# Five shared PSUM banks and joint score visits in a fused attention and expert kernel

## The chip, the cores and the metric

One core of one Trainium2 chip. The metric is the device time in microseconds (us) of a run, lower is better; beside it stands one profiled execution with a trace of every instruction.

## The reference

Attention with a memory term, then a gated expert layer on its rows, all in float32:

```
a     = softmax(q k^T / 8, causal) v              # B=4, H=8, S=576, D=64
mem   = phi(q) M_prev / (phi(q) z_prev + 1e-6)    # phi(x) = x+1 if x>0 else exp(x)
x     = sigmoid(beta) mem + (1 - sigmoid(beta)) a # -> 2304 rows x 512
out   = (sigmoid(x w_gate) * (x w_val)) w_out     # d_ff = 1536
```

## The kernel before

**Units.** The rows of x are handled in six groups of 384. Groups 1 to 4 are the first 384 rows of one batch each; groups 0 and 5 (called tail) hold the last 192 rows of two batches. A group has four pairs of heads, so there are 24 `pairs`, 0 to 23. A full pair has two items: scores of 128 queries against 256 keys, and of 384 and 128 keys together. A tail pair has three: two of 512 keys and a "mixed chunk" of 576 keys, which is done in two parts, of 320 and 256.

**Attention of a pair.** `scores` multiplies q and k on TensorE (PE) in small tiles (64x64 or 64x128 of the array, several side by side; line L523), and in the first part's banks also the memory terms phi(q) M (`terms`, L480). Such a row of small-tile matmuls among the big products is called a visit below. DVE masks the scores and takes their maximum (L587, an operation followed by a short read of its accumulator), ACT takes the exponential (L599). `turn` brings the result into key-major order: for the first eight pairs by transposes on PE (L285) and copies on ACT (L291), for the rest by a DMA transpose of two 16-bit planes, which DVE makes and joins (`planes`, L612). Of a tail pair's 512 or 576 keys a DMA transpose takes four blocks of 128; the fifth, of the mixed chunk, goes by PE transposes and an ACT copy. `values` (L282) multiplies by v for a couple of pairs, `recall` and `scaled` divide, DVE adds the memory term (`xs<-xs,xm`, L301), and `across` makes the transposed `xh` and `xl`: float32 numbers are split in two halves of PE's faster fp32r format, and each product is three matmuls.

**Experts.** `moe` runs eight stages; each step of a stage takes 128 of the 1536 columns f: 12 products of 384 columns for the gate, 12 for the value (`bank<-xh,wg`, `bank<-xh,sv`), then ACT's tanh (L920), DVE's product of gate and value (L922), the split (`gh`, `gl`), and nine products of 512 columns into three accumulators (`down`). Weights are prepared once by `convert` (ACT L810, DVE L812, L814, L817) and stored.

**Banks.** PSUM has eight banks. 0 to 2 hold the accumulators. After the first stage attention takes turns on 5, 6 and 7, and gate and value on 3 and 4.

**What sets the order.** Nothing is issued directly: the program is recorded as operations with a cost each (`pg.add`), and `issue()` schedules them in a list by these costs, by their dependencies, and by an order number, to which the table `MOVED` adds an offset for chosen operations. `block()` keeps PE operations together. The costs and the table belong to the kernel's text, and so decide the order on every engine, and which bank an operation gets is decided when it is recorded.

Of the kernel before, what the change touches and what calls it, by code (L numbers as in the profile page):

```python
# [27 lines left out]


# [174 lines left out]
def tile_attention_memory_moe(  # L204
# [60 lines left out]
    turns = {"att": 0, "gv": 0, "second": 0}  # L265
# [21 lines left out]
    def act(n, emit, r, w):  # L287
        pg.add("act", 0.09 + n / 1200.0, emit, r, w)
# [4 lines left out]
    def dve(n, emit, r, w, fast=False):  # L293
        pg.add("dve", 0.065 + n / (1920.0 if fast else 960.0), emit, r, w)
# [200 lines left out]
    def split(n):  # L495
# [10 lines left out]
        for e, (kp, kk) in enumerate(u.kp):  # L506
            for j in range(2):
# [3 lines left out]
                copy(kq[h, used], kp[h, used], used.stop, [kk], [kh])  # L511
                copy(kq[l, qs], kp[h, qs], nq, [kk], [kd])
                sub(nc.vector, kq[l, ks], kp[h, ks], kq[h, ks].bitcast(F32), nk, [kk, kh], [kl])
                q = ql[j][0][:, e * nq:(e + 1) * nq]
                sub(nc.vector, q[h], kp[h, qs], kq[h, qs].bitcast(F32), nq, [kk, kh], [kx])
# [11 lines left out]
    def scores(n, x):  # L527

        u = pairs[n]
        pair = u.tail and x == 2  # L530
        js = [slice(64 * j, 64 * j + 64) for j in range(2)]
        a = [a_r.take() for _ in js]
        if pair:
            _, q0, W = u.items[x][0]
            parts = [[(0, 0, 320)], [(0, 320, W)]]
        else:
            parts = [[(i, 0, W) for i, (_, _, W) in enumerate(u.items[x])]]
        st = [[st_r.take() for _ in js] for _ in u.items[x]]

        def part(i, cells):  # L540
            sp = [bank("att") for _ in js]
            more = pair and i == 1 or not u.tail and x == 0
            work, at = [], 0
            for y, k0, k1 in cells:
                c, q0, W = u.items[x][y]
                if pair:
                    es = [(0, 128, 0, 64), (1, 128, 64, 128)]
                    mk, mk_k = (mask2[:, :k1 - k0], "mask2") if i else (mask[:, :k1 - k0], "mask")
                else:
                    es = [(c if u.tail else 0, q0, 0, 128)]  # L550
                    if more:
                        es = [(0, q0, 0, 64), (0, q0 + 64, 64, 128)]
                    mk, mk_k = mask[:, 512 - W:], "mask"
                work.append((y, es, k0, k1, at, mk, mk_k))
                at += k1 - k0
            if more:
                u.told = [(sp[j][0][:, at:at + 3 * MC].rearrange("p (c j x) -> p c j x", c=3, j=1),
                           sp[j][1], j, j + 1) for j in range(2)]

            def together():  # L560
# [5 lines left out]
            with pg.block():  # L566
                if not divided(u) or pair:
                    e_ = {e for _, es, *_ in work for e, *_ in es}
                    pe(4 * at / 2385.0 + (0.36 if more else 0.32), together,
# [23 lines left out]
        for i, cells in enumerate(parts):  # L593
            part(i, cells)
# [283 lines left out]
    def moe(n):  # L878
# [20 lines left out]
        for at, f in enumerate(fs):  # L899
# [29 lines left out]
            if prev:  # L929
                yield from down(*prev)  # L930
# [134 lines left out]
```

## Time and profile before

| | |
|---|---|
| median of 3 runs | 610.99 us (610.62 to 611.63) |
| the profiled execution's own time | 611.24 us |
| its span | 609.5 us |
| PE busy | 598.1 us, 98% |
| DVE busy | 459.0 us, 75% |
| ACT busy | 309.9 us, 51% |
| first product of the expert layers (L278) starts | 48.25 us |
| the last one starts | 604.55 us |

Sums are made against the profiled execution; 1.7 us of its time lie outside the span. "Busy" counts the time in which an engine works on something; matmuls overlap in the pipeline, so the pace of a stretch is read from the starts of its rows, not from their lengths.

### The profile page before, as it was taken

To read this page: it belongs to the slowest core of one execution; us is meant where nothing else is said; L and a number is where in the kernel's file an instruction comes from. 1 tells how busy PE (TensorE), PEld (TensorE's weight loads), DVE (VectorE), ACT (ScalarE), POOL (GpSimd) and SP (SyncE) were. 2 spreads that over 40 slices of the span, in tenths; PEclk is the share of its full clock that TensorE was granted. 3 is DMA by queue.
4 is the path that set the end of the run, shared out by engine and by line. 5 is a ranking of instruction groups with operands and counts; after the bars stand their busy time and mean duration, and the time that the engine had idled before them with its cause. 6 is when DMAs were issued, how large, how long until landed. Compare 5 with 4: busy or idle time off the path is not lost.

```text
span 609.5 us, 13288 instructions
## 1 busy us (share of the span) xinstructions
PE 598.1 (98%) x5184; PEld 528.4 (87%) x5184; DVE 459.0 (75%) x1181; ACT 309.9 (51%) x620; POOL 8.4 (1%) x51
## 2 busy tenths in 40 slices
PE   7899999999999999999999999999999999999997
PEld 3589888888999988989888989889889888999996
DVE  4899999999998566667686867787989999333432
ACT  6987978455665232342452553463746554223332
POOL 2000000000000000000000000000000000000000
PEclk9999999999999999999999999999999999999999
DMA  8777676999594454764684653776778666222231
GB/s 319 238 230 248 188 220 215 218 242 298 150 293 157 125 136 106 154 123 108 163 168 110 131 130 95 173 185 140 154 152 202 162 123 152 48 66 90 71 103 53
DMA packets 111535, 98.17 MB, mean 161 GB/s; under 512 B 79984, under 2 KB 82032, under 8 KB 111472
## 3 DMA queue, kind: packets, MB, share of 16 engines
q1 hardware_dynamic: 111328, 97.05, 61.3%
q8 instruction: 41, 0.67, 0.5%
q10 hardware_dynamic: 144, 0.26, 0.1%
q14 instruction: 22, 0.18, 0.1%
HBM read 65.84 MB, written 12.58 MB: 129 GB/s over the span
## 4 chain that ended last, share of the span: by engine, by line
PE 94%; ACT 2%; DVE 1%; DMA 1%; SPq 1%; issue 0%; POOL 0%
PE bank L278 77%; PE bank L282 8%; PE bank L523 6%; PE bank L285 3%; PE bank L480 1%; DMA vt<-in_vp_dram 1%; ACT a L599 1%; SPq L309 1%; ACT at L291 1%; DVE a L587 0%; DVE wt L814 0%; DVE wt L817 0%; DVE xs L301 0%; DVE wt L812 0%; DVE sv L301 0%
## 5 line engine op out<-in xcount | busy, mean ns | idle before, releaser
L278 PE MATMUL bank<-xh,wg 128*128 128x384 f32 x576 | 165.2, 341 | 0.0
L278 PE MATMUL bank<-xh,sv 128*128 128x384 f32 x576 | 163.1, 338 | 0.0
L278 PE MATMUL bank<-sv,gh 128*128 128x512 f32 x432 | 139.5, 398 | 0.0
L278 PEld LDWEIGHTS bank<-xh,wg 128*128 128x128 f32 x576 | 105.5, 188 | 4.7
L278 PEld LDWEIGHTS bank<-xh,sv 128*128 128x128 f32 x576 | 105.4, 188 | 2.2 <-issue 1.0
L278 PE MATMUL bank<-xl,wg 128*128 128x384 f32 x288 | 97.4, 338 | 0.0
L278 PE MATMUL bank<-xl,sv 128*128 128x384 f32 x288 | 97.2, 338 | 0.0
L922 DVE SCALAR_TENSOR_TENSOR th<-th,bank 128x384 f32<-128x384 f32 x72 | 39.6, 550 | 76.4 <-PE bank L278 71.6
L612 DVE COPY at<-a 128x1024 uint16<-128x1024 uint16 (+1 forms) x144 | 87.0, 623 | 6.8 <-ACT a L599 3.1
L599 ACT ACTIVATE a<-a,st 128x512 f32<-128x512 f32 (+3 forms) x144 | 77.8, 582 | 26.5 <-DVE st L587 26.1
L278 PEld LDWEIGHTS bank<-sv,gh 128*128 128x128 f32 x432 | 79.2, 188 | 12.3
L920 ACT ACTIVATE th<-bank 128x384 f32<-128x384 f32 x72 | 35.3, 491 | 105.3 <-PE bank L278 102.4
L278 PE MATMUL bank<-sv,gl 128*128 128x512 f32 x216 | 84.7, 395 | 0.0
L291 ACT CAST gh<-th 128x384 fp32r<-128x384 f32 x72 | 36.9, 513 | 89.2 <-DVE th L922 88.8
L587 DVE CUSTOM_DVE_ANT_0 a<-bank,mask 128x512 f32<-128x512 f32 (+3 forms) x144 | 64.6, 483 | 20.4 <-PE bank L523 12.8
L278 PEld LDWEIGHTS bank<-xl,wg 128*128 128x128 f32 x288 | 54.1, 188 | 3.8 <-issue 1.0
L523 PE MATMUL bank<-kp 64*64 64x256 f32 (+4 forms) x416 | 51.5, 442 | 5.0 <-DMA kp<-in_qk_dram 4.1
L278 PEld LDWEIGHTS bank<-xl,sv 128*128 128x128 f32 x288 | 54.1, 188 | 1.0
L301 DVE TENSOR_TENSOR sv<-sv 128x512 fp32r<-128x512 f32 x84 | 54.3, 686 | 0.0
L301 DVE TENSOR_TENSOR gl<-th,gh 128x384 fp32r<-128x384 f32 x72 | 39.9, 554 | 16.9 <-ACT gh L291 16.8
L291 ACT CAST sv<-sv 128x512 fp32r<-128x512 f32 x84 | 47.7, 616 | 5.2 <-DMA sv<-w 5.2
L278 PEld LDWEIGHTS bank<-sv,gl 128*128 128x128 f32 x216 | 40.5, 188 | 8.8
(67 smaller groups left out, 598.2 us busy)
## 6 DMA issues: line engine op xcount, KB each, us to landing
sv<-w SPq DMA_DIRECT2D x42, 512.0 KB, 4.0
wr<-in_w_dram SPq DMA_DIRECT2D x36, 512.0 KB, 4.6
kp<-in_qk_dram SPq DMA_DIRECT2D x32, 384.0 KB, 3.7
w<-wt SPq DMA_DIRECT2D x24, 256.0 KB, 4.5
out_dram<-ob SPq DMA_DIRECT2D x14, 256.0 KB, 2.0
vt<-in_vp_dram SPq DMA_DIRECT2D x8, 330.0 KB, 4.4
vr<-in_vp_dram SPq DMA_DIRECT2D x8, 330.0 KB, 4.9
mb<-in_mz_dram SPq DMA_DIRECT2D x8, 260.0 KB, 4.7
```

Source lines behind the costliest of these rows:

```text
L278: lambda: nc.tensor.matmul(out=out, lhsT=lhsT, rhs=rhs, start=start, stop=stop), r, w)
L282: lambda: nc.tensor.matmul(out=out, lhsT=lhsT, rhs=rhs, start=start, stop=stop), r, w)
L285: pe(0.110, lambda: nc.tensor.transpose(out=out, in_=in_, identity=identity), r, w)
L291: act(n, lambda: nc.scalar.copy(out=out, in_=in_), r, w)
L301: dve(n, lambda: nc.vector.tensor_tensor(out=out, in0=in0, in1=in1, op=op), r, w)
L309: pg.add("sp", 0.5, lambda: nc.sync.dma_start(out=out, in_=in_), r, w, kb)
L523: nc.tensor.matmul(out=sp[j][0][m0:m1, at:at + k1 - k0], lhsT=kp[r, u.qa + q:u.qa + q + m1 - m0], rhs=kp[r, u.ka + k0:u.ka + k1], start=Tr ...
L587: dve(m + 10, lambda aj=aj, sj=sj, pj=pj, o=o, m=m, mk=mk, b=b0 + k0: nc.vector.tensor_tensor_reduce(out=aj[:, b:b + m], in0=pj[:, o:o + m ...
L599: act(W + 120, lambda aj=aj, sj=sj, b=b0, W=W: nc.scalar.activation(out=aj[:, b:b + W], in_=aj[:, b:b + W], func=AF.Exp, scale=-1.0, bias= ...
L612: dve(2 * W, lambda: nc.vector.tensor_copy(out=o, in_=i), r, w, fast=True)
L920: act(GT, lambda: nc.scalar.activation(out=th, in_=pg_[:, :GT], func=AF.Tanh, scale=0.5), [pg_k], [th_k])
L922: dve(GT, lambda: nc.vector.scalar_tensor_tensor(out=th, in0=th, scalar=1.0, in1=pv[:, :GT], op0=ALU.add, op1=ALU.mult,), [th_k, pv_k], [t ...
```

## The change

- `bank()` draws from one stock. From the second stage on attention, gate and value share banks 3 to 7; a list `taken` marks the two that gate and value hold until the gate's operations are recorded.
- `joint(n)` writes both items' scores and the memory terms of a full pair in one visit of 64x64 tiles, over four banks. `attn` calls it where the stock has five banks, and waits for `taken` to be empty. In the built program these are pairs 10 to 19; pairs 4 to 9 keep their two visits.
- The last four mixed chunks (pairs 20 to 23) have both parts and the terms in one visit.
- The values of a couple are one unit of the planner.
- The fifth key block of the last four pairs goes by the DMA transpose (`crossed`): eight transposes of 10x128 instead of 8x128, 16 DVE copies of 1280 instead of 1024 elements, eight pads on POOL more; eight PE transposes and four ACT copies less.
- The last 128 rows of the last step: their products are done in two halves of 256 columns in banks of their own, ACT copies the accumulator ahead, and DVE adds each half, which goes out by a DMA of its own.
- The planner's costs and the whole table `MOVED` are new, so the order is planned anew from the start.

```diff
-        ids = {"att": att_banks, "gv": [3, 4], "second": [0, 1]}[kind]
-        turns[kind] += 1
-        t, k = banks[ids[(turns[kind] - 1) % len(ids)]]
+        if kind == "second" or kind == "gv" and len(att_banks) == 3:
+            i = {"second": 0, "gv": 3}[kind] + turns[kind] % 2
+            turns[kind] += 1
+        else:
+            i = next(i for i in att_banks if i not in taken)
+            att_banks.remove(i)
+            att_banks.append(i)
+            if kind == "gv":
+                taken.append(i)
+        t, k = banks[i]
...
-        pe(0.004 + max(n, 128) / 2250.0,
+        pe(0.0055 + max(n, 128) / 2250.0,
-        pg.add("act", 0.09 + n / 1200.0, emit, r, w)
+        pg.add("act", 0.102 + n / 1200.0, emit, r, w)
-        pg.add("dve", 0.065 + n / (1920.0 if fast else 960.0), emit, r, w)
+        pg.add("dve", 0.083 + n / (1920.0 if fast else 960.0), emit, r, w)
...
+    def joint(n):
+
+        u = pairs[n]
+        js = [slice(64 * j, 64 * j + 64) for j in range(2)]
+        sp = [[bank("att") for _ in js] for _ in u.items]
...
+        for x, cells in enumerate(u.items):
+            at = 0
+            for y, (_, q, W) in enumerate(cells):
+                work.append((x, y, [(0, q, 0, 64), (0, q + 64, 64, 128)], W, at))
+                at += W
+        end = sum(W for _, _, W in u.items[0])
+
+        def together():
+            for x, _, es, W, at in work:
+                heads(u, es, sp[x], js, 0, W, at)
+            terms(u, sp[0], js, end)
...
+        plain = [job for job in jobs if not divided(u) or job[0] == 2]
+        with pg.block():
+            for some in [plain] * (n >= HP and plain != []) or [[job] for job in plain]:
...
-        n = min(nb, 4)
-        W = 128 * n
+        W = 128 * nb
...
-                scores(n, x)
+                if x == 0:
+                    pairs[n].whole = not pairs[n].tail and len(att_banks) == 5
...
+                elif not pairs[n].whole:
+                    while (taken or len(att_banks) == 3) and pairs[n].tail and x == 2:
+                        yield "wait"
+                    scores(n, (x,))
+                elif x == 0:
+                    yield from turned(1)
+                    while taken:
+                        yield "wait"
+                    joint(n)
...
+                last = g == NG - 1 and t == order[2]
+                terms = (gh, (wh, wh_k)), (gh, (wl, wl_k)), (gl, (wh, wh_k))
+                if last and f == fs[-1]:
+                    for h in (0, DM // 2):
+                        b, bk = bank("att")
+                        for i, ((l, l_k), (r, r_k)) in enumerate(terms):
+                            matmul(b[:, :DM // 2], l[:, ts], r[:, h:h + DM // 2], DM // 2, [l_k, r_k], [bk], i == 0, i == 2)
...
+                    dve(DM // 2, lambda o=o, b=b: nc.vector.scalar_tensor_tensor(
+                        out=o, in0=b[:, :DM // 2], scalar=0.5, in1=o, op0=ALU.mult, op1=ALU.add), [bk, ok], [ok])
+                    engine, queue = (("sp", nc.sync), ("act", nc.scalar))[h]
...
+        if n == 1:
+            att_banks[:] = range(3, 8)
```

PE, pair 11 (buffer `kp_106`), before: the 256-column item with its terms, and some 200 rows later the 384/128 item. Banks 63 to 65 are the accumulators, 66 and 67 gate and value, 68 to 70 attention's; each score row stands here once for its kind.

```order
L278 MATMUL bank_64<-sv_149,gl_153 128x512
L278 MATMUL bank_66<-xh_134,wg_95 128x384
L523 MATMUL bank_69<-kp_106 64x256
L523 MATMUL bank_70<-kp_106 64x256
L480 MATMUL bank_69<-mb_108,ph_128 64x65
...
L278 MATMUL bank_63<-sv_139,gh_152 128x512
L523 MATMUL bank_68<-kp_106 128x384
L523 MATMUL bank_69<-kp_106 128x384
L523 MATMUL bank_68<-kp_106 128x128
L523 MATMUL bank_69<-kp_106 128x128
L278 MATMUL bank_63<-sv_139,gh_152 128x512
```

PE, the same pair after the change. Banks 67 and 68 are those that the products of value and gate have just filled; the last gate product is the first row.

```order
L289 MATMUL bank_68<-xh_157,wg_99 128x384
L289 MATMUL bank_63<-sv_139,gh_155 128x512 x2
L289 MATMUL bank_63<-sv_139,gl_156 128x512
L289 MATMUL bank_64<-sv_139,gh_155 128x512
L534 MATMUL bank_70<-kp_106 64x256
L534 MATMUL bank_66<-kp_106 64x256
...
L534 MATMUL bank_67<-kp_106 64x384
L534 MATMUL bank_68<-kp_106 64x384
...
L534 MATMUL bank_67<-kp_106 64x128
L534 MATMUL bank_68<-kp_106 64x128
...
L491 MATMUL bank_70<-mb_108,ph_128 64x65
...
L289 MATMUL bank_64<-sv_139,gh_155 128x512
```

Both items are one piece, on banks 70 and 66 first and then on 67 and 68, three rows of products (four instructions) behind the last gate product.

DVE in the opening, before: conversions of the first weights (`wt`, lines L812, L814, L817) around the addition for pair 0 (`xs_132`). Line numbers after the change are L876, L878 and L881.

```order
L812 TENSOR_SCALAR wt_141<-wt_141 128x512
L814 SCALAR_TENSOR_TENSOR wt_141<-wr_140,wt_141 128x512
L462 SCALAR_TENSOR_TENSOR rs_133<-bank_66,ga 128x6
L817 SCALAR_TENSOR_TENSOR wt_141<-wr_140,wt_141 128x512
L466 RECIPROCAL rs_133<-rs_133 128x6
L812 TENSOR_SCALAR wt_143<-wt_143 128x512
L301 TENSOR_TENSOR xs_132<-bank_66,rs_133 128x384
L814 SCALAR_TENSOR_TENSOR wt_143<-wr_142,wt_143 128x512
L301 TENSOR_TENSOR xs_132<-xs_132,xm_126 128x384
```

After the change, from the first conversion on (line 603 is the mask of scores, 473 to 477 belong to `scaled`):

```order
L876 TENSOR_SCALAR wt_141<-wt_141 128x512
L876 TENSOR_SCALAR wt_143<-wt_143 128x512
L878 SCALAR_TENSOR_TENSOR wt_141<-wr_140,wt_141 128x512
L878 SCALAR_TENSOR_TENSOR wt_143<-wr_142,wt_143 128x512
L881 SCALAR_TENSOR_TENSOR wt_141<-wr_140,wt_141 128x512
L473 SCALAR_TENSOR_TENSOR rs_133<-bank_66,ga 128x6
L881 SCALAR_TENSOR_TENSOR wt_143<-wr_142,wt_143 128x512
L477 RECIPROCAL rs_133<-rs_133 128x6
L603 ISA a_122,st_124<-bank_68,mask 128x320
...
L312 TENSOR_TENSOR xs_132<-bank_66,rs_133 128x384
...
L312 TENSOR_TENSOR xs_132<-xs_132,xm_126 128x384
```

The conversions of two weights stand together, ahead of the mask of pair 1's mixed chunk (`a_122`), where before they stood behind it.

## Rows read from the trace of the kernel before

**Rows 1.** Page, busy time: engine, us, share of the span, instructions.

```profile
PE 598.1 (98%) x5184; PEld 528.4 (87%) x5184; DVE 459.0 (75%) x1181; ACT 309.9 (51%) x620; POOL 8.4 (1%) x51
```

**Rows 2.** Waits of PE: line, releaser, us in total, times, longest.

```profile
PE bank L523 <- DMA kp<-in_qk_dram: 4.1, 1, 4.1
```

**Rows 3.** Stretches: us, busy us of each engine, clock, DMA share, GB/s.

```profile
20.00:30.00 10.00, 8.51 (x131) 5.81 (x125) 8.80 (x22) 9.24 (x19) 0.24 (x2) 1.00 0.72 233
...
50.00:100.00 50.00, 50.00 (x593) 43.25 (x592) 48.37 (x145) 39.80 (x85) 0.67 (x6) 1.00 0.73 221
...
410.00:510.00 100.00, 100.00 (x977) 87.71 (x976) 91.94 (x221) 52.68 (x100) 0.70 (x6) 1.00 0.72 156
```

**Rows 4.** PE's timeline by start and us: a 256-column score visit among products.

```profile
218.01 0.52 PE L278 MATMUL bank<-xh,wg 128*128 128x384 f32 x2
218.46 0.66 PE L523 MATMUL bank<-kp 64*64 64x256 f32 x8
...
219.40 0.44 PE L278 MATMUL bank<-xl,wg 128*128 128x384 f32 x1
219.68 0.51 PE L278 MATMUL bank<-xh,wg 128*128 128x384 f32 x2
...
220.03 0.33 PE L278 MATMUL bank<-xl,wg 128*128 128x384 f32 x1
```

**Rows 5.** The same: a 384/128-column score visit.

```profile
242.03 0.39 PE L278 MATMUL bank<-sv,gl 128*128 128x512 f32 x1
242.35 1.14 PE L523 MATMUL bank<-kp 64*128 64x384 f32 x8
243.41 0.44 PE L278 MATMUL bank<-xh,wg 128*128 128x384 f32 x1
243.70 0.33 PE L278 MATMUL bank<-xl,wg 128*128 128x384 f32 x1
```

**Rows 6.** The same: a 320-column score visit.

```profile
452.05 0.34 PE L278 MATMUL bank<-xl,sv 128*128 128x384 f32 x1
452.31 0.77 PE L523 MATMUL bank<-kp 64*64 64x320 f32 x8
453.01 0.61 PE L278 MATMUL bank<-xh,sv 128*128 128x384 f32 x2
```

**Rows 7.** The same, in the opening: a merged mixed chunk, the next transposes.

```profile
40.27 1.20 PE L523 MATMUL bank<-kp 64*64 64x320 f32 x16
...
41.75 0.44 PE L285 MATMUL bank<-idn,a 128*128 128x128 f32 x2
```

**Rows 8.** The same, in the last group: two lone transposes among products.

```profile
515.52 0.39 PE L278 MATMUL bank<-sv,gh 128*128 128x512 f32 x1
515.75 0.27 PE L285 MATMUL bank<-idn,a 128*128 128x128 f32 x1
...
516.43 0.63 PE L278 MATMUL bank<-sv,gh 128*128 128x512 f32 x2
```

**Rows 9.** Groups by line and shape: count, busy us, mean ns, idle before.

```profile
L612 DVE COPY at<-a 128x1024 uint16<-128x1024 uint16 x96 | 66.9, 717 | 4.0 <-ACT a L599 3.1 <-DMA a<-at 0.5
...
L920 ACT ACTIVATE th<-bank 128x384 f32<-128x384 f32 x72 | 35.3, 491 | 105.3 <-PE bank L278 102.4 <-DVE gl L301 2.5
...
L814 DVE SCALAR_TENSOR_TENSOR wt<-wr,wt 128x512 int32<-128x512 int32 x36 | 24.6, 685 | 0.4
```

**Rows 10.** DVE's timeline in the opening; idle before and its releaser in brackets.

```profile
21.67 0.43 DVE L812 TENSOR_SCALAR wt<-wt 128x512 int32<-128x512 int32 x1 [1.16 <-ACT wt L810]
...
45.11 0.56 DVE L454 SCALAR_TENSOR_TENSOR ph<-kp,ph 128x384 f32<-128x384 f32 x1 [0.77 <-ACT ph L452]
...
48.92 0.55 DVE L301 TENSOR_TENSOR xs<-xs,xm 128x384 f32<-128x384 f32 x1
```

**Rows 11.** Timeline of all engines at the end; ACTq is ACT's DMA queue.

```profile
604.29 0.69 DVE L949 TENSOR_SCALAR at<-bank 128x512 f32<-128x512 f32 x1 [1.68 <-PE bank L278]
...
605.60 0.38 ACTq L953 DMA_DIRECT2D out_dram<-at  x1
```

More of the change, by code (lines that the diff above doesn't have):

```diff
@@ L525, in heads, with scores @@
                     rhs=kp[r, u.ka + k0:u.ka + k1], start=True, stop=True)
-    def scores(n, x):
+    def scores(n, xs):
         u = pairs[n]
-        pair = u.tail and x == 2
         js = [slice(64 * j, 64 * j + 64) for j in range(2)]
[L532 to L560, printed above, removed]
@@ L561, in together @@
+        told = u.told
+        def together(jobs):
+            for _, _, sp, more, work, at in jobs:
                 for _, es, k0, k1, o, _, _ in work:
@@ L564, in together @@
                     terms(u, sp, js, at)
[L566 to L569, printed above, removed]
-                       [u.kp[e][1] for e in e_] + (u.ph_k + [k for _, mk in mem[u.g] for k in mk] if more else []),
-                       [sp[j][1] for j in range(2)])
-                else:
-                    (_, es, k0, k1, _, _, _), = work
-                    m = k1 - k0
-                    for j in range(2):
-                        kq, kk, ql, kx = u.kq[j][es[0][0]]
-                        keys = kq[:, u.ka + k0:u.ka + k1]
-                        out, out_k = sp[j][0][:, :m], sp[j][1]
-                        q = es[0][1]
-                        matmul(out, kq[:, u.qa + q:u.qa + q + 128], keys, m, kk, [out_k], True, False)
-                        matmul(out, ql[:, q:q + 128], keys, m, kk + kx, [out_k], False, True)
+        plain = [job for job in jobs if not divided(u) or job[0] == 2]
@@ new lines, in scores @@
+        with pg.block():
+            for some in [plain] * (n >= HP and plain != []) or [[job] for job in plain]:
+                more = any(job[3] for job in some)
+                e_ = {e for *_, work, _ in some for _, es, *_ in work for e, *_ in es}
+                pe(4 * (sum(job[5] for job in some) + 3 * MC * more) / 2385.0 + 0.34, lambda some=some: together(some),
+                   [u.kp[e][1] for e in e_] + (u.ph_k + [k for _, mk in mem[u.g] for k in mk] if more else []),
+                   [k for _, _, sp, *_ in some for _, k in sp])
+            for _, _, sp, _, work, _ in [job for job in jobs if job not in plain]:
+                (_, es, k0, k1, _, _, _), = work
+                m = k1 - k0
+                for j in range(2):
+                    kq, kk, ql, kx = u.kq[j][es[0][0]]
+                    keys = kq[:, u.ka + k0:u.ka + k1]
+                    out, out_k = sp[j][0][:, :m], sp[j][1]
+                    q = es[0][1]
+                    matmul(out, kq[:, u.qa + q:u.qa + q + 128], keys, m, kk, [out_k], True, False)
+                    matmul(out, ql[:, q:q + 128], keys, m, kk + kx, [out_k], False, True)
@@ L739, in attn, with turned @@
         late, held = [], []
-        def over():
-            while held and freed:
-                across(held.pop(0))
-                yield
-        for n, x in [(n, x) for n in range(NP) for x in range(len(pairs[n].items))] + [(NP, 0)]:
-            if n < NP:
-                last = len(pairs[n].items) - 1
-                yield from over()
-                while held and n == 2 * HP + HP - 1:
-                    yield "wait"
-                    yield from over()
-                scores(n, x)
-                late.append((n, x))
-                yield
-                if x == 0:
-                    if n == 0:
-                        gates()
-                    if n and n + 1 < NP and pairs[n + 1].tail:
-                        load_pair(n + 1)
-                    yield
-                if x == last:
-                    if n + 2 < NP and not pairs[n + 2].tail:
-                        load_pair(n + 2)
-                    feature(n + 1)
-                    split(n + 1)
-                    yield
-            while len(late) > (SKEW if n < HP else n < NP):
+        def turned(most):
+            while len(late) > most:
                 k, x = late.pop(0)
@@ L791, in attn, with over @@
                     yield ("group", pairs[k].g) if k % HP == HP - 1 else None
+        def over():
+            while held and freed:
+                across(held.pop(0))
+                yield
+        for n, x in [(n, x) for n in range(NP) for x in range(len(pairs[n].items))] + [(NP, 0)]:
+            if n < NP:
+                last = len(pairs[n].items) - 1
+                yield from over()
+                while held and n == 2 * HP + HP - 1:
+                    yield "wait"
+                    yield from over()
+                if x == 0:
+                    pairs[n].whole = not pairs[n].tail and len(att_banks) == 5
+                if not pairs[n].whole and BOTH and n < HP:
+                    if x == 0:
+                        yield from turned(1)
+                    if x != 1:
+                        scores(n, [(0, 1), (2,)][x // 2])
+                elif not pairs[n].whole:
[3 more added lines that the diff above has]
+                elif x == 0:
+                    yield from turned(1)
+                    while taken:
+                        yield "wait"
+                    joint(n)
+                late.append((n, x))
+                yield
+                if x == 0:
+                    if n == 0:
+                        gates()
+                    if n and n + 1 < NP and pairs[n + 1].tail:
+                        load_pair(n + 1)
+                    yield
+                if x == last:
+                    if n + 2 < NP and not pairs[n + 2].tail:
+                        load_pair(n + 2)
+                    feature(n + 1)
+                    split(n + 1)
+                    yield
+            yield from turned(SKEW if n < HP else n < NP)
     scratch = [dram.tile([128, 2, DM], F32, name=f"w{f}") for f in range(NF)]
@@ L881, in moe @@
         prev = None
-        accs = []
+        accs, ends, early = [], [], []
         order = (2, 0, 1) if g in (0, NG - 1) else range(GT // 128)
@@ L928, in moe @@
             gate()
+            for i in taken:
+                att_banks.remove(i)
+                att_banks.append(i)
+            taken.clear()
             if prev:
                 yield from down(*prev)
+            if g == NG - 1 and f == fs[-1]:
+                ob, ob_k = at_r.take()
+                early.extend((ob, [ob_k + (h,) for h in range(2)]))
+                act(DM, lambda ob=ob: nc.scalar.activation(
+                    out=ob[:, :DM], in_=accs[order[2]][0], func=AF.Copy, scale=0.5), [accs[order[2]][1]], early[1])
             weights(firsts[n] + at + 2)
```

170 lines of the change are left out of this document (109 added, 61 removed), and 83 rows, old and new, of the table MOVED.

## The prediction

> **What bounds the kernel now.** I read the page first. PE is busy for 98% of the span [rows 1], so a change counts by the work it takes from PE, by the waits it puts before PE, or by the time before PE gets going. The waits of PE come next: the longest is 4.1 us at the very start, for the first keys [rows 2]; the other three that the view lists are 0.9 us each. A table of stretches then says where another engine is near its limit. DVE is full from 20 to 100 us (8.80 of 10, 48.37 of 50 us), and nearly so from 410 to 510 (91.94 of 100), yet PE loses 1.5 us in the first of these and nothing in the other two [rows 3]. The first product of the expert layers starts at 48.25 us, the last at 604.55; between them PE's instructions follow each other without a gap worth naming. So there I sum PE's work, and only the opening is a matter of other engines.
>
> **Price of a score visit.** A product of 384 columns takes 0.175 us from its start to the next one's: two from 219.68 to 220.03 [rows 4]. By its columns one of 512 takes 0.233. From 218.01 to 219.68 stand three products of 384 and one visit of 64x64 tiles with the 256-column scores and the memory terms; so the visit costs 1.67 - 0.525 = 1.15 us, of which 0.10 lies ahead of its first matmul (218.01 + 0.35 = 218.36 to 218.46) and 0.11 behind, where the product after it takes 0.28 instead of 0.175. The visit with 384 and 128 columns takes 1.67 - 0.233 - 0.175 = 1.26 [rows 5]. A 320-column visit takes 453.01 - 452.05 - 0.175 = 0.79, and 0.11 behind it: 0.90 [rows 6].
> In the opening one merged visit stands already: 320, 256 and the terms in 1.48 us, between transposes [rows 7]. With 0.10 ahead and 0.11 behind it would be 1.69 among products. It streams 8x320 + 8x256 + 24x65 = 6168 columns (the row's 16 are eight of either width; the trace has two records for each matmul in float32, so 24 for the twelve of the terms), the 256-column visit 8x256 + 24x65 = 3608: 0.54 us for 2560 columns, 0.21 us for a thousand. The fixed part of a visit is then 1.15 - 0.76 = 0.39, and that of the 320-column visit 0.90 - 0.54 = 0.36. The 384/128 visit on 64x128 tiles streams 2048 columns on two tiles, as much time as 4096 on four: 0.86, with 0.40 fixed. So moving it to 64x64 costs nothing, and what a merge saves is one fixed part.
>
> **The change, part by part.**
> Joint visits: the order shows ten (pairs 10 to 19; pairs 4 to 9 keep two). One costs 1.15 + 0.86 = 2.01 for 1.15 + 1.26 = 2.41 apart: 10 x 0.40 = 4.0 us less, 4.1 with unrounded visits.
> Last four mixed chunks: 1.69 for 0.90 + 1.15: 4 x 0.36 = 1.4 less.
> Fifth key blocks of the last four pairs: eight transposes leave PE. From 515.52 to 516.43 stand three 512-column products and two lone transposes: 0.91 - 0.70 = 0.21, 0.11 each [rows 8]; 8 x 0.11 = 0.9 less. In exchange 16 DVE copies grow from 1024 to 1280 elements; by the 0.717 us of the short form [rows 9] that is at most 16 x 0.18 = 2.9 us of DVE in the stretch in which it has 8 us to spare, and PE never waited for the last group's attention in the old trace. I cost it at nothing; without that cover PE would wait for it late, 2.9 us at most. The eight DMA transposes grow too, with no new ones on SP; the eight pads hide on POOL, which is busy for 0.70 us of that stretch [rows 3]. Four ACT copies go.
> Values of a couple as one unit: they stood together in the old order too, so nothing.
> The old trace does not show a merge among products. From below I bound it by the 0.11 behind a visit alone (14 x 0.11 = 1.5 instead of 5.5), from above by the fixed parts (5.5). I take the upper one, since three visits of different tiles and columns agree on 0.36 to 0.40 and a lone transpose, which keeps the products' 128x128 tile, has next to no fixed part: 0.11 us in all. The Trainium skill, "TensorEngine Tiling (Array Packing)", Key Properties, says that a change of the tiling mode drains TensorE; by it a merge would save a whole way in and out, as the fixed parts here do.
> All PE work after 48.25 us: -6.4.
>
> Opening: the whole order is planned anew, and PE's set of instructions before the first product is the same. Here DVE decides. The xs addition at 48.92 us [rows 10] is needed by the transposes that go with the eighth product. In the new order five more weight-conversion steps and one more split stand ahead of it; three of 0.685 us [rows 9], two of 0.43 (the length of the one at 21.67) and the split, as long as the three, are 3.6 us, and 3.2 less the 0.07 by which such steps overlap. Waits can take them up: DVE waited 1.16 us for ACT at 21.67, and 0.77 at 45.11 [rows 10]. If both are filled, 1.3 us stay; if only the second, 2.4; if the added steps all fall into idle time, nothing. The excerpt shows the moved steps early, ahead of the mixed chunk's scores, near the first wait. I take +1.2, from 0 to 2.5.
>
> New waits behind 48.25: a joint visit takes four of the five shared banks, one or two of which a gate or value product has just left. In the excerpt for pair 11 four 512-column products (0.93 us) separate the last gate product and the visit; 0.10 of entry and the 256-column scores in the two other banks (0.43) come before the first write into the bank in question. Needed are the product's own tail (0.17), tanh on ACT (0.491 [rows 9]) and the product of gate and value on DVE (384 columns of two operands, 0.55 like the addition of [rows 10]): 1.21 against 1.46. If both engines are free at once, none waits; 0.3 us in all for the ten.
>
> End: today ACT copies the last tile and issues its output at 605.60 [rows 11]. Now the halves wait for DVE, which first copies another tile (from 604.29 on for 0.69) and then adds 256 columns twice at about 0.4 each (half that copy's columns and some start): the second ends at 605.8 and is issued by 605.9. The half-size transfers give that back. 0.0, from -0.3 to +0.3.
>
> Sum: profiled execution 611.24 - 6.4 + 1.2 + 0.3 = 606.3; the median of the runs is 0.25 below that execution, so **606.1**.
>
> **Rivals.** 0.2%, 1.2 us, is about what a measurement of this kernel can tell from no change.
> 1. As summed, with 0.5 to 2.5 us given back in the opening: 604.6 to 607.4. Chance 0.60.
> 2. The opening gives nothing back or gains: with the added steps in idle time and first conversions that stand 2.5 us of DVE earlier, 603.4 to 604.6. For it: PE has only 1.5 us idle there between 20 and 30. Against: DVE is the full engine. 0.17.
> 3. Joint visits wait a little: the slack of 0.25 is short, and an ACT cast or a DVE copy that has just begun (0.5 to 0.7) uses it up. At 0.13 to 0.37 us for each of ten: 607.4 to 609.8. For it: one stock makes the gate's next products need what a visit holds. Against: DVE is busy for 75% of the span [rows 1] and for more in the stretches of [rows 3], so for less in between, where most of these visits lie. 0.11.
> 4. The change does not do what it says: a merge saves only the gap behind a visit. Then 610.99 - 1.5 - 0.9 + 1.5 (opening and new waits) gives 610.1, no change. Against: the three fixed parts. 0.06.
> 5. Slower: the banks couple attention to the gates. A visit that wants four of five banks waits for tanh and the gate product, and the next gate's products wait for the scores' masks and the recall that read the visit's four banks. It turns at 0.61 us of waiting for each visit (6.1 / 10, on a slack of 0.25: 0.86 us of delay); with a full ACT cast and a DVE copy ahead of the two steps (0.6 + 0.7 - 0.25 = 1.05 us) it gives 606.1 + 10.5 = 616.6. Against: PE never waited for these steps in the old trace, and the visits lie where DVE is least busy. 0.06. The Trainium skill names this risk ("TensorEngine Tiling (Array Packing)", PSUM Bottleneck: tiling makes TensorE faster and not the emptying of PSUM); no row of this kernel shows it yet.
>
> **How the numbers follow.** The likeliest case is 606.1, its own range 604.6 to 607.4. Cases 1 to 3 hold 0.88; the ends are cut inside cases 2 and 3, at 603.4 and 609.2, which leaves out the slower cases and a little on each side: 0.84 and, with the doubt in the bounds themselves, 0.8. Faster by over 0.2% (below 609.8): 0.88. Within: 0.07. Slower: 0.05.
>
> **What would show it.** In the new profile the joint visits last 2.0 us from product to product and the merged chunks 1.7; the products keep 0.175 and 0.233; the first product starts at 48 to 50 us and the last at about 599. PE's waits list nothing for DVE or ACT above 0.5 us after the opening. The prediction is wrong if a joint visit starts late with a wait for the gate's readers ahead of it, if the visits last over 2.3, if the first product comes later than 51, or if PE waits for DVE's longer copies between 410 and 510.

## The result and the profile after

The changed kernel takes 604.82 us (median of four runs, 604.23 to 605.47), the kernel before beside it 611.12: ratio 0.9901, 95% interval 0.9889 to 0.9913, so 6.3 us less. The prediction was 606.1, its likeliest case 604.6 to 607.4. The profiled execution took 605.47 us with a span of 603.7; it is the slowest of the four, and a stall that it shows is the likely reason (below).

The page of the changed kernel, and the waits of PE (line, releaser, us in total, times, longest):

```profile
span 603.7 us, 13415 instructions
...
PE 592.5 (98%) x5259; PEld 527.5 (87%) x5259; DVE 458.4 (76%) x1183; ACT 309.1 (51%) x616; POOL 9.5 (2%) x59
```

```profile
PE bank L534 <- DMA kp<-in_qk_dram: 3.9, 1, 3.9
PE bank L491 <- issue: 1.1, 1, 1.1
PE bank L296 <- ACT a L612: 0.5, 1, 0.5
PE bank L296 <- ACT at L302: 0.5, 1, 0.5
PE bank L296 <- DVE st L603: 0.2, 1, 0.2
```

As before [rows 1], PE is busy for 98%; there are no waits in the list from the expert layers, and none for a bank that a gate's reader holds. One row is new: 1.1 us for "issue", which names nothing that the profile shows. PE's timeline has a joint visit and a merged mixed chunk (start, us):

```profile
203.67 0.39 PE L289 MATMUL bank<-sv,gh 128*128 128x512 f32 x1
203.98 1.53 PE L534 MATMUL bank<-kp 64*64 64x256 f32 x24
205.33 0.53 PE L491 MATMUL bank<-mb,ph 64*64 64x65 f32 x24
205.79 0.50 PE L289 MATMUL bank<-sv,gh 128*128 128x512 f32 x1
206.12 0.40 PE L289 MATMUL bank<-sv,gl 128*128 128x512 f32 x1
...
442.66 0.51 PE L289 MATMUL bank<-xh,sv 128*128 128x384 f32 x2
443.10 1.20 PE L534 MATMUL bank<-kp 64*64 64x320 f32 x16
...
444.58 0.73 PE L289 MATMUL bank<-sv,gh 128*128 128x512 f32 x2
445.15 0.34 PE L289 MATMUL bank<-xl,sv 128*128 128x384 f32 x1
```

From 203.67 to 206.12 stand two products of 512 columns (0.23 each) and the joint visit: 2.45 - 0.46 = 1.99 us, where the two visits of [rows 4, 5] took 2.41. From 442.66 to 445.15 stand two products of 384, two of 512 and the mixed chunk: 2.49 - 0.35 - 0.46 = 1.68, where the visits of [rows 4, 6] took 2.05. All ten joint visits take 1.99 to 2.01 us, all four mixed chunks 1.68.

I sum the same over the whole of PE's timeline from the first expert product to the last: each product at its pace (0.1745 us for 384 columns, 0.2315 for 512), and for all else the time between the products around it, less their pace.

| | before | after |
|---|---|---|
| first product starts, us | 48.25 | 48.68 |
| products | 459.0 | 459.0 |
| all else that PE does between products | 96.8 in 70 stretches | 90.0 in 49 |
| gaps between products | 0.8 | 1.0 |
| last product starts | 604.55 | 598.53 |
| from there to the end of the span | 4.90 | 5.13 |

(The last product has 512 columns before and 256 after, which makes 0.11 of the difference between the starts. The last row is from the unrounded times, 609.45 - 604.55 and 603.65 - 598.53.)

### The profile page after: what moved, and what is told of

Its sections match the earlier page's. It is cut to its first block, busy times and chain, and to the rows that moved or that the text cites. A ratio compares the mean times of both kernels' runs of the same rounds, so it can differ in the third digit from the quotient of the medians.

```text
span 603.7 us, 13415 instructions
## 1 busy us (share of the span) xinstructions
PE 592.5 (98%) x5259; PEld 527.5 (87%) x5259; DVE 458.4 (76%) x1183; ACT 309.1 (51%) x616; POOL 9.5 (2%) x59
## 4 chain that ended last, share of the span: by engine, by line
PE 93%; DVE 3%; ACT 1%; issue 1%; DMA 1%; DVEq 0%
PE bank L289 77%; PE bank L732 8%; PE bank L534 5%; PE bank L296 2%; PE bank L491 1%; DVE a L603 1%; ACT a L612 1%; DMA kp<-in_qk_dram 1%; ACT at L302 0%; DVE ph L465 0%; DVE xs L312 0%; DVE wt L878 0%; DVE wg L312 0%; DVE sv L312 0%; DVE xm L312 0%
## 5 line engine op out<-in xcount | busy, mean ns | idle before, releaser
L289 PE MATMUL bank<-xh,wg 128*128 128x384 f32 x576 | 162.0, 338 | 0.0
L289 PE MATMUL bank<-sv,gh 128*128 128x512 f32 x434 | 141.1, 396 | 0.0
L662 DVE COPY at<-a 128x1024 uint16<-128x1024 uint16 (+2 forms) x144 | 87.4, 640 | 0.8 <-DMA a<-at 0.4
L289 PE MATMUL bank<-sv,gl 128*128 128x512 f32 (+1 forms) x217 | 85.2, 395 | 0.0
L612 ACT ACTIVATE a<-a,st 128x512 f32<-128x512 f32 (+4 forms) x84 | 50.4, 640 | 16.5 <-DVE st L603 16.2
L302 ACT CAST sv<-sv 128x512 fp32r<-128x512 f32 x84 | 47.8, 616 | 9.9 <-DMA sv<-w 9.8
L534 PE MATMUL bank<-kp 64*64 64x256 f32 (+5 forms) x496 | 48.0, 423 | 3.9 <-DMA kp<-in_qk_dram 3.9
L603 DVE CUSTOM_DVE_ANT_0 a<-bank,mask 128x512 f32<-128x512 f32 (+4 forms) x84 | 42.2, 531 | 9.6 <-PE bank L534 8.2
```

What stands on the lines that cost most here:

```text
L302: act(n, lambda: nc.scalar.copy(out=out, in_=in_), r, w)
L534: nc.tensor.matmul(out=sp[j][0][m0:m1, at:at + k1 - k0], lhsT=kp[r, u.qa + q:u.qa + q + m1 - m0], rhs=kp[r, u.ka + k0:u.ka + k1], start=Tr ...
L603: dve(m + 10, lambda aj=aj, sj=sj, pj=pj, o=o, m=m, mk=mk, b=b0 + k0, i=i: nc.vector.tensor_tensor_reduce(out=aj[:, b:b + m], in0=pj[:, o: ...
L612: act(W + 120, lambda aj=aj, sj=sj, b=b0, W=W, d=depth[x]: nc.scalar.activation(out=aj[:, b:b + W], in_=aj[:, b:b + W], func=AF.Exp, scale ...
L662: dve(2 * W, lambda: nc.vector.tensor_copy(out=o, in_=i), r, w, fast=True)
```

## The experiments

All are the changed kernel with one edit, its order kept as it was but for the edit, unless told otherwise; each has its name in brackets, and `...` in an edit stands for lines left out. Beside them the kernel before measured 610.5 to 610.7 us, beside the changed kernel itself 611.12; so a time against 604.82 is uncertain by half a microsecond, and where less is asked the sums over PE's timeline decide. In the edits `moves` is the list of operations in the order in which the planner issues them.

**What a merge saves.** The joint visits in two pieces of the same tiles, with one product between them (`joints_apart`):

```diff
...
-        def together():
-            for x, _, es, W, at in work:
-                heads(u, es, sp[x], js, 0, W, at)
-            terms(u, sp[0], js, end)
+        def some(part):
+            for x, _, es, W, at in work:
+                if x == part:
+                    heads(u, es, sp[x], js, 0, W, at)
+            if part == 0:
+                terms(u, sp[0], js, end)
+
+        together = lambda: some(0), lambda: some(1)
```

The second piece is issued behind the next product on PE.

> The changed kernel with its order, but each of the ten joint visits is issued as two of the same 64x64 tiles, with one 512-column product between them. Theory (a merge saves one fixed part of 0.36 to 0.40 us): each pair of visits takes 2.41 us instead of 2.00, the time is 4.0 us longer, 608.8. Rival (only the gap behind a visit is saved, or nothing): 0 to 1.1 us longer, at most 605.9.

608.61 us, 3.8 longer. Its timeline at the same place:

```profile
203.02 0.39 PE L301 MATMUL bank<-sv,gh 128*128 128x512 f32 x1
203.34 0.66 PE L546 MATMUL bank<-kp 64*64 64x256 f32 x8
...
204.28 0.50 PE L301 MATMUL bank<-sv,gh 128*128 128x512 f32 x1
204.71 1.09 PE L546 MATMUL bank<-kp 64*64 64x384 f32 x16
205.74 0.50 PE L301 MATMUL bank<-sv,gl 128*128 128x512 f32 x1
```

From 203.02 to 205.74 two products and both visits but for the last 0.10 behind: 2.72 - 0.46 + 0.10 = 2.36 us instead of 2.00. A merge saves 0.36. On PE's timeline the run is 4.3 us longer, 3.6 by the ten visits and 0.7 by a wait of another kind: at 211.64 the product put between the pieces stands 0.62 us for DVE, which is still reading its accumulator (`ob`).

The mixed chunks apart as well (`all_apart`; the two pieces again go out with one product between):

```diff
...
-                pe(4 * (sum(job[5] for job in some) + 3 * MC * more) / 2385.0 + 0.34, lambda some=some: together(some),
+                pe(4 * (sum(job[5] for job in some) + 3 * MC * more) / 2385.0 + 0.34, (lambda some=some: together(some)) if len(some) == 1 else (lambda some=some: together(some[:1]), lambda some=some: together(some[1:])),
```

> The same, and also the last four mixed chunks as two visits with one product between. Theory: 4.0 + 4 x 0.36 = 5.4 us longer, 610.2: what is left of the gain over the kernel before is the fifth key blocks and noise of the new order. Rival: below 606.3.

609.76 us, 1.15 more than the last one; each mixed chunk takes 0.79 + 1.24 = 2.03 instead of 1.68, four times 0.36 on PE. With the fourteen merges undone, 0.8 us are left to the kernel before (610.59 beside this run), or 1.5 without the wait at the accumulator, which stands in this run too: 0.9 for the fifth key blocks, and the form of the visits' second halves (next).

**Which way costs.** The visit in one piece, its second half on the tiles that it had in the kernel before (`two_shapes`):

```diff
-                work.append((x, y, [(0, q, 0, 64), (0, q + 64, 64, 128)], W, at))
+                work.append((x, y, [(0, q, 0, 128)] if x else [(0, q, 0, 64), (0, q + 64, 64, 128)], W, at))
```

> The changed kernel, but inside the joint visit the scores of 384 and 128 columns stand on 64x128 tiles, as in the kernel before; the visit stays one piece. Theory A (the fixed part belongs to the way between products and small tiles alone): the visit stays 2.00 us, no change, 604.8. Theory B (every change of the tile shape has its price, and the terms behind change it back): two more changes inside, 0.1 to 0.4 us a visit, 1 to 4 us longer.

608.93 us, 4.1 longer (3.65 on PE's timeline): theory B, at its upper end.

```profile
202.96 0.39 PE L289 MATMUL bank<-sv,gh 128*128 128x512 f32 x1
203.27 1.73 PE L534 MATMUL bank<-kp 64*64 64x256 f32 x16
204.93 0.58 PE L491 MATMUL bank<-mb,ph 64*64 64x65 f32 x24
205.44 0.50 PE L289 MATMUL bank<-sv,gh 128*128 128x512 f32 x1
205.78 0.40 PE L289 MATMUL bank<-sv,gl 128*128 128x512 f32 x1
```

2.82 - 0.46 = 2.36 us, 0.36 more, with no product in between. Some 0.05 of it belongs to the form: a 384/128 visit of its own takes 1.27 on 64x128 tiles and, in the run with the joint visits apart, 2.36 - 1.14 = 1.22 on 64x64 (1.14 for the 256-column visit). The other 0.31 are two changes of the tile shape inside the visit, nearly as much as the 0.36 of a way out to the products and back. So the fixed part of a visit is two changes of shape at 0.16 to 0.18 us, and the joint visit gains because all of it stands on one shape. That agrees with the Trainium skill, "TensorEngine Tiling (Array Packing)", Key Properties: a change of the tiling mode, not of the tile, drains TensorE. Of this the runs show the price, 0.16 to 0.18 us for each change, and not the draining itself.

What the time goes into is therefore open. In the changed kernel the weights of a product are loaded while the product ahead is running (from 203.43 for the one at 203.67), but at both changes of shape the load starts only with the row itself (203.98 and 205.79). A load that does not go ahead may be part of the price or all of it; no run tells it from a draining.

**Whether banks couple visits and gates.** In the trace of the changed kernel the last reader of a joint visit's banks is a gate's tanh, which ends 0.81 to 1.01 us before the visit writes its bank in nine cases; in the tenth it is DVE's memory term, 0.92 before. For the visit at 203.98 it is this one, which ends at 203.67; the visit reaches the bank with the first 384 columns, at 204.47:

```profile
203.18 0.49 ACT L992 ACTIVATE th<-bank 128x384 f32<-128x384 f32 x1 [0.77 <-PE bank L289]
```

The tanh of those steps four times over (`tanh_late`):

```diff
...
+        for i in self.close:
+            for d in ops[i][4]:
+                if ops[d][0] == "act" and d in self.tanh:
+                    k = next(k for k, m in enumerate(moves) if m[1] == d)
+                    moves[k + 1:k + 1] = [moves[k]] * 3
...
```

> The changed kernel, but each tanh whose bank a joint visit takes next is computed four times over on ACT, which frees the bank about 1.35 us later (three more at 0.45 each). Theory (the banks couple the visits to the gates; in the trace of the changed kernel the second half of a visit starts 0.81 to 1.01 us behind the tanh, so this is its slack): each of the ten visits waits about 0.3 to 0.5 us, 3 to 5 us in all, 608 to 610. Rival (something else holds the visit, the bank has more time): PE shows no such wait, 604.8.

614.51 us, 9.7 longer, twice the upper end of what I expected. Its timeline:

```profile
203.04 2.06 ACT L1009 ACTIVATE th<-bank 128x384 f32<-128x384 f32 x4 [0.77 <-PE bank L304]
...
203.53 0.39 PE L304 MATMUL bank<-sv,gh 128*128 128x512 f32 x1
...
203.85 1.85 PE L549 MATMUL bank<-kp 64*64 64x256 f32 x15
...
206.52 0.50 PE L304 MATMUL bank<-sv,gh 128*128 128x512 f32 x1
...
206.86 0.40 PE L304 MATMUL bank<-sv,gl 128*128 128x512 f32 x1
```

3.33 - 0.46 = 2.87 us instead of 2.00. Nine of the ten visits wait, for 0.67 to 0.87 us, the tenth (whose last reader is DVE) keeps 2.00: 6.9 us in all. The tanh ends 1.57 us later; less a slack of 0.8 that is the wait. Another 2 us are gaps among the products, mostly behind late casts on ACT (1.19 us at 383, 0.63 at 235). These make 8.9 of the 9.7; the profiled execution, 613.41, is the fastest of the four. So the coupling of rival 5 is real, and the changed kernel stays clear of it by less than one microsecond.

**Fifth key blocks.** By PE transposes again (`fifth_by_pe`):

```diff
...
-        W = 128 * nb
+        n = min(nb, 4)
+        W = 128 * n
...
+        if nb > n:
...
+            tp, tk = bank("att")
+            for j, (t, ks, ak) in enumerate(a):
+                transpose(tp[:, j * 128:j * 128 + 128], t[:, W:W + 128], idn,
+                          ks + ["idn", ak + ("pad",)], [tk])
...
```

> The changed kernel with the fifth key blocks of the last four pairs as before: eight PE transposes and four ACT copies, DMA transposes of four blocks, DVE copies of 1024 elements. Theory: 8 x 0.11 = 0.9 us longer, 605.7. Rival (DVE, 93% busy between 410 and 510 us, held PE up there after the change): the 2.3 us of DVE that go away make up for it, 604.8 or below.

606.53 us, 1.7 longer. On PE the eight transposes cost 0.9 (90.9 us between products instead of 90.0). The rest is one wait of 0.9 us at 220.7 us, far from the edit: a `gh` cast on ACT queued behind the casts of reloaded weights, whose DMA took 6.9 us from issue to landing instead of 5.0 in the changed kernel:

```profile
219.09 1.14 ACT L309 CAST sv<-sv 128x512 fp32r<-128x512 f32 x2 [1.53 <-DMA sv<-w]
220.13 0.51 ACT L309 CAST gh<-th 128x384 fp32r<-128x384 f32 x1
```

The rival (DVE's longer copies cost as much) falls: without them PE wins nothing back.

**The opening.** One step of the first conversion three times (`dve_more`):

```diff
...
+        k = next(k for k, m in enumerate(moves) if m[1] in self.first)
+        moves[k + 1:k + 1] = [moves[k]] * 2
...
```

> The changed kernel; one step of the first weight conversion on DVE is done three times instead of once, 1.3 us more of DVE work at about 20 us and nothing else. Theory of the prediction (DVE sets when the expert products start): the first product comes about 1.2 us later, at 49.9, and the time is 606.0. Rival (PE's own work and the waits for others set it, DVE has idle time to give): the first product moves by less than 0.4 us, 604.8 to 605.2.

605.92 us, and the first product at 49.28. Of the seven executions with an unchanged opening that were profiled, five start it at 47.5 to 47.8 and two at 48.7 to 48.8, those with PE's "issue" wait. So it comes 1.5 to 1.75 later than in the five, but 0.2 to 0.5 of that stands ahead of the edit already: DVE's mask just before it starts at 16.81 here, at 16.35 to 16.60 in the five. From that mask to the first product it is 32.47 us instead of 31.18 to 31.20. So 1.3 us of DVE work move the first product by 1.3: DVE does set it.

The first six conversion steps, with what depends on them, behind the addition for pair 0 (`convert_late`):

```diff
...
+        first = [i for i in line if i in self.conv][:6]
+        goal = next(k for k, m in enumerate(moves) if m[1] in self.adds)
+        held = set(first)
+        for i in line:
+            if any(d in held for d in ops[i][4]):
+                held.add(i)
+        early = [m for m in moves[:goal + 1] if m[1] in held]
...
+        moves = [m for m in moves[:goal + 1] if m[1] not in held] + early + moves[goal + 1:]
...
```

> The changed kernel, but the first six weight-conversion steps on DVE, which it does from 17.6 to 21.0 us, stand behind the addition for pair 0, about where the kernel before had them. Theory (these steps fill DVE's idle time while PE is in the values of pair 0; DVE is full behind it): DVE stands from 17.6 to 20.2 us, the first expert product comes 2 to 3 us later than the 47.6 of the runs without PE's stall at 21 us, at 49.6 to 50.6, and the time is 606.5 to 607.5. Rival (the addition for pair 0, which now comes 0.9 us sooner, is what the opening waits for): first product at 46.7 to 47.6, 604 to 605.

609.80 us, 5.0 longer, and the first product at 52.73, 5.1 later and not 2 to 3. DVE's idle row, ACT's and PE's:

```profile
20.53 0.17 DVE L488 SCALAR_TENSOR_TENSOR rs<-bank,ga 128x6 f32<-128x6 f32 x1 [2.57 <-PE bank L747]
```

```profile
25.66 0.62 ACT L317 CAST wg<-wt 128x512 fp32r<-128x512 f32 x1 [2.84 <-DVE wt L900]
26.26 0.62 ACT L317 CAST sv<-wt 128x512 fp32r<-128x512 f32 x1
26.79 0.77 ACT L627 ACTIVATE a<-a,st 128x576 f32<-128x576 f32 x1
```

```profile
PE bank L311 <- ACT a L627: 4.8, 3, 3.9
```

DVE stands for 2.57 us as expected. But two casts of the converted weights stand in ACT's queue ahead of the exponential that PE's transposes need, and wait for the conversions: ACT stands for 2.84 and PE for 3.9. I had counted one engine and missed the queue behind it. TensorE's clock adds to it. Behind PE's wait the granted clock (the column before the DMA share) is 0.50, which is 1.2 GHz; from 20 to 25 us it was 1.00, 2.4 GHz:

```profile
27.60:30.00 2.40, 2.39 (x11) 2.06 (x13) 1.74 (x7) 2.40 (x7) 0.00 (x0) 0.50 0.99 359
```

The transposes and scores from 27.61 to 31.35 take 3.74 us; the same rows of the two-shape run take 2.67, from 23.31 to 25.98. So 1.1 of the 5 us are the clock's.

**The table.** Both kernels without their tables of offsets (`no_table_after`, `no_table_before`):

```diff
-MOVED = {
...
-}
+MOVED = {}
```

> The changed kernel without its table of offsets, ordered by the planner's costs and dependencies alone. Theory (the merges save PE work in any order): PE's work behind the first product stays as it is, about 549 us with the visits, and every longer time is in waits; I expect 5 to 20 us of them, 610 to 625.

> The kernel before without its table, likewise: 616 to 631. Theory: the difference to the changed kernel without a table is about the 6 us of saved PE work, give or take the waits of either. Rival (the gain comes from the new table, not from the merges): without tables the two differ by less than 2 us.

614.02 us (611.3 to 616.6, the profiled execution the slowest) and 624.14. PE's work between products is 93.2 us in 49 stretches, of which 3.0 are one joint visit's wait, against 97.2 in 71. Without that wait it is 7.0 us less, with the tables 6.8: the saving on PE does not come from the new table. The times themselves differ by 10 us, and that is no measure of the merges, since the rest is waits and clock. The first products start at 55.1 and 51.4, and the run of the kernel before has a wait of 4.7 us for `xh`, behind which the granted clock is 0.51:

```profile
543.00:548.00 5.00, 5.00 (x15) 4.57 (x16) 1.57 (x3) 1.00 (x2) 0.00 (x0) 0.51 0.00 0
```

There a product of 384 columns takes 0.32 us instead of 0.1745, about 2.5 us more in all. The changed kernel without its table has such stretches too, from 17 to 23.5 us (0.50) and from 226 to 228, behind the joint visit's wait (0.50).

**Further merges and the tail.** Joint visits for pairs 5 to 9 too (`joints_early`: the stock of five banks from the first stage on, the table carried over operation by operation):

```diff
...
-        if n == 1:
+        if n == 0:
             att_banks[:] = range(3, 8)
```

> The changed kernel with the stock of five banks from the first stage on, so that pairs 5 to 9 have joint visits too; the table of offsets is carried over operation by operation, without a search for a new one. Theory (each merge saves 0.36 us, and a visit's banks are free when it comes): 5 x 0.36 = 1.8 us less, 603.0. Rival (between 50 and 150 us DVE is busy for 93% and empties the banks late, so four banks at once make PE wait): the visits there wait 0.5 us or more each, 605 or longer, waits of PE on DVE in that stretch.

612.41 us, slower than both the changed kernel and the kernel before (610.65 beside it). The visits cost about 2.0 there as well (2.26 the longest), but:

```profile
65.86 2.50 ACT L628 ACTIVATE a<-a,st 128x256 f32<-128x256 f32 x6
...
68.26 0.47 ACT L969 ACTIVATE th<-bank 128x384 f32<-128x384 f32 x1
```

```profile
68.78 1.22 PE L266 MATMUL bank<-sv,gh 128*128 128x512 f32 x2 [2.76 <-ACT th L969]
```

A joint visit makes six exponentials ready at once; they stand ahead of the next tanh, and PE waits 2.76 us for it. Behind this wait the granted clock is 0.52, and the 512-column product at 69.80 takes 0.43 us instead of 0.23:

```profile
68.78:72.00 3.22, 3.21 (x10) 2.54 (x11) 3.22 (x8) 2.43 (x5) 0.00 (x0) 0.52 0.47 153
```

At half the clock these 3.2 us do the work of 1.6, so I estimate 1.6 us for the clock. A second wait of 2.06 us for DVE ends at 79.29; DVE is busy throughout from 76 to 80. PE's timeline is 7.2 us longer in all, 9.2 with the 2.0 that five merges should save; the 2.8 that these three do not cover were not traced. With a table searched for this order it might come out otherwise; that was not tried.

Both halves of the last tile on ACT's queue (`tail_act`):

```diff
-                    engine, queue = (("sp", nc.sync), ("act", nc.scalar))[h]
+                    engine, queue = "act", nc.scalar
```

> The changed kernel, but both halves of the last tile are issued on ACT's DMA queue; in the changed kernel the first half's issue on SP begins at 599.93, behind three others, the second's on ACT at 599.58. Theory (the end is set by the issue that waits on SP): from the last product to the end of the span 4.6 to 4.9 us instead of 5.2, 0.3 to 0.6 us less in the time, no more than a trace can show. Rival (the transfers themselves set the end): 5.2.

605.15 us, no difference. The end of the changed kernel, and of this one:

```profile
598.53 0.28 PE L289 MATMUL bank<-sv,gl 128*128 128x256 f32 x1
...
599.58 0.38 ACTq L1024 DMA_DIRECT2D out_dram<-at  x1
599.93 0.70 SPq L1024 DMA_DIRECT2D out_dram<-at  x1
```

```profile
598.44 0.28 PE L289 MATMUL bank<-sv,gl 128*128 128x256 f32 x1
...
599.11 0.89 ACTq L1024 DMA_DIRECT2D out_dram<-at  x2
```

From the last product's start the last issue now ends after 1.56 us (599.11 + 0.89 - 598.44) instead of 2.10 (599.93 + 0.70 - 598.53), but the span still ends 5.26 us behind that start, 5.13 in the changed kernel. So without the issue on SP the end comes no sooner, as the rival has it. One thing speaks against calling the matter closed: in five other runs whose end is that of the changed kernel (`joints_apart`, `all_apart`, `fifth_by_pe`, `no_table_after`, `joints_early`) that issue took 0.44 to 0.45 us instead of 0.70, and the span ended 4.8 us behind the last product's start. Why they differ no run shows; the end varies by 0.3 us with it.

## Why the prediction was right, point by point

| term | predicted | measured |
|---|---|---|
| ten joint visits | -4.0 (4.1 unrounded) | 2.00 for 2.41: -4.1, of which 3.6 by the merge and 0.5 by the form of the second half |
| four mixed chunks | -1.4 | 1.68 for 2.05: -1.5 |
| fifth key blocks | -0.9 | -0.9 |
| other stretches on PE | 0 | -0.3 (what is left of 96.8 - 90.0; one old 256-column visit, at 484 us, took 1.44 instead of 1.14) |
| opening | +1.2 | +0.4 in the profiled execution, -0.6 without PE's stall |
| new waits | +0.3 | +0.2 |
| end | 0.0 | +0.2 (it varies by 0.3) |

The price of a visit held to 0.01 us. The fixed part, read from three old visits and a merged one in the opening, was 0.04 too high for the joint visits (0.36 come back when a merge is undone), and "moving it to 64x64 costs nothing" was 0.05 too low. That the two make up for each other, so that the price came out to 0.01, is luck. The lower bound (only the gap behind a visit) and rival 4 fall with joints_apart and all_apart. The two-shape run says more than the prediction did: the fixed part is not bound to the large products but to any change of shape.

**The step that was mis-sized is the opening.** "If both are filled, 1.3 us stay; ... if the added steps all fall into idle time, nothing. ... I take +1.2, from 0 to 2.5." The mechanism stood (dve_more: DVE decides), the size and the sign did not. I looked for idle time at the two waits of [rows 10], 1.9 us. In the two-shape run, which has the same opening and no stall of PE, DVE does 41.38 us of work by 50 us where the kernel before does 38.44; the stretch from 0 to 50 us (busy us of PE, its weight loads, DVE, ACT), before and in that run:

```profile
0.00:50.00 50.00, 43.15 (x624) 30.66 (x625) 38.44 (x130) 41.51 (x82) 3.70 (x25) 1.00 0.77 265
```

```profile
0.00:50.00 50.00, 44.79 (x629) 31.31 (x629) 41.38 (x136) 44.17 (x87) 3.77 (x25) 1.00 0.79 277
```

So 2.9 us of idle time are filled, and the additions come sooner for it, the first at 22.29 instead of 24.98 and the one of [rows 10] at 48.35 instead of 48.92 (the kernel before, then the two-shape run):

```profile
24.98 0.55 DVE L301 TENSOR_TENSOR xs<-xs,xm 128x384 f32<-128x384 f32 x1
```

```profile
22.29 0.56 DVE L312 TENSOR_TENSOR xs<-xs,xm 128x384 f32<-128x384 f32 x1
...
48.35 0.55 DVE L312 TENSOR_TENSOR xs<-xs,xm 128x384 f32<-128x384 f32 x1
```

The conversions moved to 17.6 us, while PE is in the values of pair 0 and DVE had nothing to do; convert_late shows what losing that place costs in this order, 5 us, of which 1.1 are the clock's. So rival 2 describes the opening, though the time lies in the range of case 1, by 0.2 us. The bound of zero from below was wrong: steps that start earlier also take the engines behind them along.

**The slack of a joint visit** was read too short, 0.25 us: I put tanh and the product of gate and value between the last gate product and the visit. The bank in question is the gate's, which only tanh reads. For pair 11 the value of the same step is written behind the visit, to another bank, and that of the step before, in the visit's other bank, was read 2.6 us earlier. With the prediction's own numbers that leaves 1.46 - 0.17 - 0.49 = 0.80; measured are 0.8 to 1.0, no visit waits, and rivals 3 and 5 did not come. Their mechanism is there, as tanh_late shows.

DVE's longer copies were hidden as costed: between 410 and 510 us DVE is busy for 93.15 us, 91.94 before [rows 3], and PE for all 100:

```profile
410.00:510.00 100.00, 100.00 (x918) 89.86 (x919) 93.15 (x219) 51.85 (x97) 2.66 (x12) 1.00 0.71 164
```

For the end I gave a range of 0.3 either way, which holds.

The profiled execution is 0.65 us above the median. PE's stall at 21 us (1.1 us, in two of seven profiles with the same opening) accounts for more than that; without it a late weight reload can take as much back at 220 us, as in fifth_by_pe and in tail_act (a gap of 0.84 us there). Which of them the three executions without a trace had is not known.

## What to carry to other kernels

Price a small-tile stretch among large products by two lines of the timeline, with the products in between taken off, and separate the columns from the fixed part by comparing stretches of different lengths; then count changes of tile shape, not instructions, and merge only what can stand on one shape. In the cases seen here, a unit that needs many banks at once is free as long as its last reader is done before it writes, and waits for whatever delay goes beyond that: measure that slack in time, and name the reader by the bank. Where an engine is full, look for idle time over the whole stretch ahead, not only next to the moved step, and follow the queue of the next engine as well. Where PE has stood, look at the granted clock behind the wait before you put the whole loss down to the wait.

## What the runs showed of the hardware that I had not expected

- Two changes of shape within small tiles (64x64 to 64x128 and back) cost 0.31 us, nearly as much as the 0.36 for going from 128x128 to 64x64 and back.
- PE stood for 1.1 us in the middle of a row of memory-term matmuls at 21 us in two of seven executions whose instructions are the same up to there, and in the other five not. The profile names no releaser; the cause stays open.
- The same weight reload, in kernels that are alike up to there, took 5.0 us from issue to landing in one execution and 6.7 and 6.9 in two others, where PE stood 0.84 and 1.05 us at 220 us for a cast that stood behind it.
- In four runs the granted clock fell from 1.00 to 0.50 (2.4 to 1.2 GHz) behind waits of PE: of 2.76 us (joints_early), 3.9 (convert_late), 4.7 (no_table_before), 3.0 and, in its opening, 1.5 and 0.9 (no_table_after). Work behind them then took up to 1.9 times its usual time.
